# Moving the weight transfers behind the first chunk's loads, overlapping the first chunk's pieces, and multiplying by rms_g after the transpose, in a fused retention and SwiGLU kernel

## The chip, the cores and the metric

One core of a Trainium2 chip. The metric is the time of one execution on the device, in microseconds (us). The kernel before takes 300.7 us. Every run below ran on one core, beside runs of the kernel before on the same chip.

## The reference

Two operations in a row: a retention recurrence over 4 batches, 8 heads and 768 positions, then an RMS norm and a SwiGLU feed-forward network (FFN) on the 3072 rows that it gives.

```python
# attention part: B=4, H=8, S=768, D=64
for t in range(S):
    state = gamma[h] * state + outer(k[t], v[t])
    y[t] = scale * q[t] @ state
# FFN part: x is y as 3072 rows of 512; d_ff = 1536
xn  = x / sqrt(mean(x*x) + 1e-6) * rms_g
out = (silu(xn @ w_gate) * (xn @ w_val)) @ w_out
```

## The kernel before

In the views of the profile PE is TensorE, ACT is ScalarE, DVE is VectorE, POOL is GpSimd and SP is SyncE; SPq is the queue of transfers that SP issues. The sequence is cut into six chunks of 128 positions. For a chunk and a batch there are five pieces:

- **cast:** q and k to bf16, v times a decay (vp).
- **T:** transposes of q and k, and their copy out of PSUM (qkT).
- **A:** scores and the causal mask (am).
- **Y:** output and state.
- **X:** normalise (xn), transpose (xt), copy into xnT.

FFN c works on the four batches of chunk c. It has 16 slots: twelve gate and value blocks gv(n), then four down projections down(b). The pieces of chunk c+1 are emitted between these slots. The traces show each engine at its instructions in the order of emission (in experiment 12 an instruction whose input was there at 21.85 us began at 27.67, behind one that waited for its load), so the plan of slots *is* the schedule.

```python
for b in range(B):
    load(0, b)                       # q, k, v of chunk 0: 12 transfers on SP
...
g_bc = const.tile([128, DM], F32, name="g_bc")
nc.sync.dma_start(out=g_bc, in_=moe_rms_g.partition_broadcast(128))
...
for i in range(DFF // WB):           # all weights, at once, on GpSimd (fp32 in DRAM, bf16 in the tiles)
    nc.gpsimd.dma_start(out=wg_b[:, :, sl], in_=wg_v[:, :, sl])
    nc.gpsimd.dma_start(out=wv_b[:, :, sl], in_=wv_v[:, :, sl])
for i in range(3):
    nc.gpsimd.dma_start(out=wo_b[:, sl, :], in_=wo_v[:, sl, :])
...
def piece_x(c, b):
    nc.vector.scalar_tensor_tensor(out=xn, in0=x, scalar=rstd[:, b:b + 1], in1=g_bc,
                                   op0=ALU.mult, op1=ALU.mult)
    for s in range(KS):
        nc.tensor.transpose(xt_ps[:, s, :], xn[:, s * 128:(s + 1) * 128], ident)
    nc.vector.tensor_copy(xnT[:, :, b * C:(b + 1) * C], xt_ps)

def attention(c):                    # slots of FFN c-1 behind which each piece of chunk c stands
    for b in range(B):
        s[2 * b].append(lambda b=b: cast(c, b))
        s[2 * b + 1].append(lambda b=b: piece_t(c, b))
        s[2 * b + 2].append(lambda b=b: piece_a(c, b))
        s[2 * b + 3].append(lambda b=b: piece_y(c, b))
        s[12 + b].append(lambda b=b: piece_x(c, b))
    s[10].append(lambda: piece_rstd(c))    # one rstd for the four batches
...
for sl in attention(0):              # chunk 0 has no FFN beside it
    for f in sl: f()
for c in range(NCH):                 # FFN c with the pieces of chunk c+1
    ...
```

## Time and profile before

The three executions took 300.64, 300.68 and 300.84 us. The beginnings of the FFNs, taken from PE's instructions in order of time (the first g_ps matmul of each chunk), divide the profiled span of 299.4 us:

| stretch | from | length, us | what limits it |
|---|---|---|---|
| start (chunk 0's pieces) | 0 | 59.26 | transfers to 42, then a serial chain |
| FFN 0 | 59.26 | 42.99 | PE, with slow first matmuls (four fours in 6.00 us, 3.47 in FFN 1) |
| FFN 1 | 102.25 | 40.47 | PE |
| FFN 2 | 142.72 | 40.52 | PE |
| FFN 3 | 183.24 | 40.53 | PE |
| FFN 4 | 223.77 | 40.30 | PE |
| FFN 5 (no pieces beside it) | 264.07 | 35.33 | PE |

How the lines behind the table are read is told in the prediction.

### The profile page before, as it was taken

What the parts mean: (1) busy time and instruction counts of PE and PEld (TensorE: products, weight loads), DVE (VectorE), ACT (ScalarE), POOL (GpSimd) and SP (SyncE); (2) the same over time, 40 slices, a digit from 0 to 9 for tenths busy, and PEclk for the clock granted to TensorE, in tenths of its full rate; (3) what the DMA queues carried; (4) which work ended last, traced back from release to release, by engine and by line L of the source; (5) the groups of instructions that cost most, each with busy time, mean ns of one, the idle gap of its engine ahead of it and who ended that gap; (6) DMA issues with size and microseconds to landing.
All of it is one profiled execution on the core that took longest, in us unless ns stands there. A gap on an engine that the chain in (4) does not pass through costs nothing.

```text
span 299.4 us, 4437 instructions
## 1 busy us (share of the span) xinstructions
PE 242.3 (81%) x1696; PEld 122.8 (41%) x1696; DVE 141.1 (47%) x232; ACT 100.0 (33%) x186; POOL 91.2 (30%) x153
## 2 busy tenths in 40 slices
PE   0025212399999999999999999999999999999994
PEld 0014111145544454544454444545444444544441
DVE  0006405617765266873376653577544556424300
ACT  5012212034452245431445313544224453233321
POOL 8472245403337006281035350161921101000000
PEclk9999999999999999999999999999999999999999
DMA  8999999992400498002793025970110000110012
GB/s 164 191 191 192 196 197 227 219 218 44 96 3 35 129 228 171 2 0 105 182 225 53 0 73 137 219 136 1 36 71 36 2 0 2 70 70 2 1 47 93
DMA packets 84310, 30.43 MB, mean 102 GB/s; under 512 B 75457, under 2 KB 81089, under 8 KB 84289
## 3 DMA queue, kind: packets, MB, share of 16 engines
q1 hardware_dynamic: 78480, 25.43, 41.0%
q0 software_dynamic: 5808, 4.72, 9.8%
q8 instruction: 13, 0.21, 0.3%
q14 instruction: 9, 0.07, 0.1%
HBM read 28.57 MB, written 6.29 MB: 116 GB/s over the span
## 4 chain that ended last, share of the span: by engine, by line
PE 53%; DVE 17%; ACT 9%; SPq 8%; DMA 6%; issue 5%; POOL 1%; DVEq 0%; ACTq 0%; POOLq 0%
PE o_ps L259 21%; PE g_ps L248 13%; PE v_ps L251 12%; SPq L62 8%; DVE am L158 7%; DMA k_f<-in_k_dram 6%; DVE hT L254 4%; ACT xsq L188 3%; DVE x L185 3%; ACT qkT L144 3%; ACT sg L253 3%; PE xt_ps L218 2%; PE y_ps L171 2%; DVE xn L213 1%; DVE xnT L219 1%
## 5 line engine op out<-in xcount | busy, mean ns | idle before, releaser
L254 DVE TENSOR_TENSOR hT<-sg,v_ps 128x512 bf16<-128x512 bf16 x72 | 49.5, 688 | 72.5 <-PE v_ps L251 45.4
L248 PE MATMUL g_ps<-xnT,wg_b 128*128 128x512 bf16 x288 | 75.9, 387 | 3.1 <-DVE xnT L219 3.1
L251 PE MATMUL v_ps<-xnT,wv_b 128*128 128x512 bf16 x288 | 74.9, 383 | 0.0
L259 PE MATMUL o_ps<-wo_b,hT 128*128 128x512 bf16 x288 | 65.6, 379 | 0.0
L253 ACT ACTIVATE sg<-g_ps 128x512 bf16<-128x512 f32 x72 | 43.0, 597 | 63.9 <-PE g_ps L248 63.9
L198 POOL CAST st_b<-st_f 64x256 bf16<-64x256 f32 x40 | 15.9, 397 | 110.6 <-DVE st_f L197 102.5
L158 DVE TENSOR_TENSOR am<-a_ps,causal 128x512 bf16<-128x512 f32 x48 | 30.8, 682 | 33.5 <-PE a_ps L154 33.5
L251 PEld LDWEIGHTS <-wv_b 128*128 128x128 bf16 x288 | 28.5, 99 | 35.0 <-issue 1.7
L259 PEld LDWEIGHTS <-hT 128*128 128x128 bf16 x288 | 27.5, 98 | 30.4
L248 PEld LDWEIGHTS <-wg_b 128*128 128x128 bf16 x288 | 25.5, 99 | 29.1 <-DVE xnT L219 3.5
L262 ACT COPY o_sb<-o_ps 128x512 f32<-128x512 f32 x24 | 14.1, 586 | 56.5 <-PE o_ps L259 56.5
L144 ACT COPY qkT<-qk_ps 128x1024 bf16<-128x1024 bf16 x24 | 23.9, 998 | 25.0 <-PE qk_ps L142 25.0
L188 ACT ACTIVATE xsq<-x 128x512 f32<-128x512 bf16 x24 | 15.1, 630 | 49.4 <-DVE x L185 47.7
L142 PE MATMUL qk_ps<-ident,qb 128*128 128x128 bf16 x96 | 10.2, 234 | 24.4 <-POOL qb L129 24.4
L131 POOL TENSOR_TENSOR vp<-v_f,vdec 128x512 bf16<-128x512 f32 x24 | 26.8, 1117 | 8.7 <-DMA v_f<-in_v_dram 5.5
L219 DVE COPY xnT<-xt_ps 128x512 bf16<-128x512 bf16 x24 | 10.2, 425 | 31.4 <-PE xt_ps L218 31.4
L213 DVE SCALAR_TENSOR_TENSOR xn<-x,rstd,g_bc 128x512 bf16<-128x512 bf16 x24 | 23.5, 980 | 1.9 <-POOL rstd L207 1.9
L129 POOL CAST qb<-q_f 128x512 bf16<-128x512 f32 x24 | 17.0, 707 | 14.4 <-issue 8.8
L171 PE MATMUL y_ps<-vp,am 128*128 128x64 bf16 x192 | 13.6, 202 | 8.7 <-DVE am L158 5.9
L185 DVE TENSOR_TENSOR x<-y_ps,ydec 128x512 bf16<-128x512 f32 x24 | 16.6, 690 | 4.7 <-PE y_ps L171 4.1
L142 PEld LDWEIGHTS <-qb 128*128 128x128 bf16 x96 | 7.1, 105 | 25.8 <-POOL qb L129 24.6
L218 PE MATMUL xt_ps<-ident,xn 128*128 128x128 bf16 x96 | 10.2, 234 | 8.7 <-DVE xn L213 8.7
(38 smaller groups left out, 140.2 us busy)
## 6 DMA issues: line engine op xcount, KB each, us to landing
q_f<-in_q_dram SPq DMA_DIRECT2D x24, 256.0 KB, 4.8
k_f<-in_k_dram SPq DMA_DIRECT2D x24, 256.0 KB, 4.9
v_f<-in_v_dram SPq DMA_DIRECT2D x24, 256.0 KB, 4.9
out_dram<-o_sb SPq DMA_DIRECT2D x24, 256.0 KB, 2.0
wg_b<-in_moe_w_gate_dram POOLq DMA_DIRECT2D x4, 384.0 KB, 13.4
wv_b<-in_moe_w_val_dram POOLq DMA_DIRECT2D x4, 384.0 KB, 15.5
wo_b<-in_moe_w_out_dram POOLq DMA_DIRECT2D x3, 512.0 KB, 23.0
g_bc<-in_moe_rms_g_dram SPq DMA_DIRECT2D x1, 256.0 KB, 8.1
```

The source lines that it names most:

```text
L62: nc.sync.dma_start(out=x, in_=src[b].rearrange("h (c p) d -> c p h d", p=C)[c])
L131: nc.gpsimd.tensor_tensor(out=vp, in0=v_f, in1=vdec[:, c, :, None].to_broadcast([128, H, D]), op=ALU.mult)
L144: nc.scalar.copy(qkT, qk_ps)
L158: nc.vector.tensor_tensor(out=am[:, i], in0=a_ps[i], in1=causal[:, None, :].to_broadcast([128, NHP, 128]), op=ALU.mult)
L185: nc.vector.tensor_tensor(out=x, in0=y_ps, in1=ydec[:, c, :, None].to_broadcast([128, H, D]), op=ALU.mult)
L188: nc.scalar.activation(xsq, x.rearrange("p h d -> p (h d)"), AF.Square, accum_out=cur[c, "ssq"][:, b:b + 1])
L213: nc.vector.scalar_tensor_tensor(out=xn, in0=x.rearrange("p h d -> p (h d)"), scalar=cur[c, "rstd"][:, b:b + 1], in1=g_bc, op0=ALU.mult, o ...
L248: nc.tensor.matmul(g_ps, wg_b[:, s, sl], xnT[:, s, :], start=s == 0, stop=s == KS - 1)
L251: nc.tensor.matmul(v_ps, wv_b[:, s, sl], xnT[:, s, :], start=s == 0, stop=s == KS - 1)
L253: nc.scalar.activation(sg, g_ps, AF.Silu)
L254: nc.vector.tensor_tensor(out=hT[:, n, :], in0=sg, in1=v_ps, op=ALU.mult)
L259: nc.tensor.matmul(o_ps, hT[:, n, b * C:(b + 1) * C], wo_b[:, n, :], start=n == 0, stop=n == NFF - 1)
```

## The change

The intent has three parts. **Transfers:** the weights wait until chunk 0's loads are partly in (a block behind each batch's cast, the rest behind all of chunk 0), and chunk 1's loads wait for the first silus of FFN 0. **Overlap:** chunk 0's pieces are interleaved across batches, rstd is made per batch, and chunks 1 to 5 get new slots for their pieces. **rms_g:** the multiply by g moves from xn to the copy of xT out of PSUM, where g is one number per partition. Eight matmuls without a use ("hot") stand ahead of FFN 0, so that PE's slow stretch falls on them.

```diff
-    for i in range(DFF // WB):          # all weights at once
+    def load_w(i):                      # one gate and one value block
...
+        if c == 0 and b > 0:            # in cast(): a block behind the casts of batches 1, 2, 3
+            load_w(b - 1)
-        if c + 1 < NCH:
+        if 0 < c < NCH - 1:
             load(c + 1, b)
...
-        x = work.tile([128, H, D], BF16, name="x", bufs=5)
+        x = work.tile([128, H, D], F32, name="x", bufs=5)
...
-        nc.vector.scalar_tensor_tensor(
-            out=xn, in0=x..., scalar=cur[c, "rstd"][:, b:b + 1], in1=g_bc, op0=ALU.mult, op1=ALU.mult)
+        nc.vector.tensor_scalar_mul(xn, d["x"]..., d["rstd"])
...
-        nc.vector.tensor_copy(cur[c, "xnT"][:, :, b * C:(b + 1) * C], xt_ps)
+        nc.vector.tensor_tensor(out=cur[c, "xnT"][:, :, b * C:(b + 1) * C], in0=xt_ps,
+            in1=g_col[:, :, None].to_broadcast([128, KS, 128]), op=ALU.mult)
...
+    PLAN = dict(cast=(0, 2, 4, 6), t=(1, 3, 5, 7), a=(2, 4, 6, 8), y=(3, 5, 7, 9), x=(9, 11, 13, 14))
+    PLAN1 = dict(cast=(6, 7, 9, 11), t=(7, 9, 11, 13), a=(8, 10, 12, 14), y=(9, 11, 13, 15), x=(13, 14, 15, 15))
...
-    for sl in attention(0):
-        for f in sl: f()
+    for step in "C0 T0 C1 A0 T1 Y0 C2 A1 T2 X0 Y1 C3 A2 T3 X1 Y2 A3 X2 Y3".split():
+        P[step[0]](0, int(step[1]))
+    for i in range(3, DFF // WB): load_w(i)
+    for i in range(3): load_wo(i)
+    hot = fps.tile([128, GT], F32, name="hot", tag="ff")
+    for i in range(8):
+        nc.tensor.matmul(hot, ident, st_b[0]..., start=True, stop=True)
+    piece_x(0, 3)
...
+            if c == 0 and i < B:
+                load(1, i, after=mark[0, i])     # behind the silu of block i
```

Left out of this excerpt: in chunk 0 the qb casts and st_f copies move to ACT, the load buffers go from five to six, an early Silu brings the table load (1.28 us, at 48.73 before) forward, and four small transfers on ACT's queue replace the 256 KB one of g_bc.

More of the change, by code (lines that the diff above doesn't have):

```diff
@@ L45 @@
     const = ctx.enter_context(tc.tile_pool(name="const", bufs=1))
-    loads = ctx.enter_context(tc.tile_pool(name="loads", bufs=5))
+    loads = ctx.enter_context(tc.tile_pool(name="loads", bufs=6))
     work = ctx.enter_context(tc.tile_pool(name="work", bufs=3))
@@ L53, with load @@
     out_v = out.rearrange("(b c p) m -> c b p m", b=B, p=C)
+    SYNC_DEP = mybir.DependencyInfo(mybir.DependencyClass.Sync, mybir.DependencyReason.DATA)
     raw = {}
-    def load(c, b):
+    def load(c, b, after=None):
         t = []
@@ L61, in load @@
             x = loads.tile([128, H, D], F32, name=name)
-            nc.sync.dma_start(
+            i = nc.sync.dma_start(
                 out=x, in_=src[b].rearrange("h (c p) d -> c p h d", p=C)[c])
+            if after is not None:
+                tc.add_manual_dep(i.ins, after.ins.name, SYNC_DEP, reason="transfer order")
             t.append(x)
@@ L91 @@
         nc.scalar.activation(ydec[:, :, h], pos_f, AF.Exp, scale=lng[h], bias=lnscale)
-    eps4 = const.tile([128, B], F32, name="eps4")
-    nc.gpsimd.memset(eps4, 1e-6)
-    mhalf4 = const.tile([128, B], F32, name="mhalf4")
-    nc.gpsimd.memset(mhalf4, -0.5)
-    g_bc = const.tile([128, DM], F32, name="g_bc")
-    nc.sync.dma_start(out=g_bc, in_=moe_rms_g.partition_broadcast(128))
+    mhalf = const.tile([128, 1], F32, name="mhalf")
+    nc.gpsimd.memset(mhalf, -0.5)
+    warm = const.tile([128, 1], F32, name="warm")
+    nc.scalar.activation(warm, zero, AF.Silu)
+    g_col = const.tile([128, KS], F32, name="g_col")
+    for s in range(KS):
+        nc.scalar.dma_start(out=g_col[:, s:s + 1], in_=moe_rms_g[s * 128:(s + 1) * 128][:, None])
     st_f = [const.tile([128, NHP, D], F32, name=f"st_f{b}") for b in range(B)]
@@ L116, with load_wo @@
         nc.gpsimd.dma_start(out=wv_b[:, :, sl], in_=wv_v[:, :, sl])
-    for i in range(3):
+    def load_wo(i):
         sl = slice(i * 4, (i + 1) * 4)
@@ L122 @@
     cur = {}
+    mark = {}
     def cast(c, b):
@@ L128, in cast @@
         vp = work.tile([128, H, D], BF16, name="vp")
-        nc.gpsimd.tensor_copy(qb, q_f.rearrange("p h d -> p (h d)"))
+        if c == 0:
+            nc.scalar.copy(qb, q_f.rearrange("p h d -> p (h d)"))
+        else:
+            nc.gpsimd.tensor_copy(qb, q_f.rearrange("p h d -> p (h d)"))
         nc.gpsimd.tensor_copy(kb, k_f.rearrange("p h d -> p (h d)"))
@@ L187, in piece_y @@
         xsq = work.tile([128, DM], F32, name="xsq")
+        ssq = work.tile([128, 1], F32, name="ssq")
         nc.scalar.activation(xsq, x.rearrange("p h d -> p (h d)"), AF.Square,
-                             accum_out=cur[c, "ssq"][:, b:b + 1])
+                             accum_out=ssq)
+        d["ssq"] = ssq
+        piece_rstd(c, b)
         if c < NCH - 1:
@@ L194, in piece_y @@
                 if c == 0:
-                    nc.vector.tensor_copy(st_f[b][r], kv)
+                    nc.scalar.copy(st_f[b][r], kv)
                 else:
@@ L199, in piece_y, with piece_rstd @@
         d["x"] = x
-    def piece_rstd(c):
-        ssq = cur[c, "ssq"]
-        ms = work.tile([128, B], F32, name="ms")
-        nc.gpsimd.tensor_scalar(out=ms, in0=ssq, scalar1=1.0 / DM, scalar2=1e-6,
+    def piece_rstd(c, b):
+        ms = work.tile([128, 1], F32, name="ms")
+        nc.gpsimd.tensor_scalar(out=ms, in0=cur[c, b]["ssq"], scalar1=1.0 / DM, scalar2=1e-6,
                                 op0=ALU.mult, op1=ALU.add)
-        rstd = work.tile([128, B], F32, name="rstd")
-        nc.gpsimd.tensor_tensor(out=rstd, in0=ms, in1=mhalf4, op=ALU.pow)
-        cur[c, "rstd"] = rstd
+        rstd = work.tile([128, 1], F32, name="rstd")
+        nc.gpsimd.tensor_tensor(out=rstd, in0=ms, in1=mhalf, op=ALU.pow)
+        cur[c, b]["rstd"] = rstd
     def piece_x(c, b):
-        x = cur.pop((c, b))["x"]
+        d = cur.pop((c, b))
         xn = work.tile([128, DM], BF16, name="xn")
-        nc.vector.scalar_tensor_tensor(
-            out=xn, in0=x.rearrange("p h d -> p (h d)"), scalar=cur[c, "rstd"][:, b:b + 1],
-            in1=g_bc, op0=ALU.mult, op1=ALU.mult)
+        nc.vector.tensor_scalar_mul(xn, d["x"].rearrange("p h d -> p (h d)"), d["rstd"])
         xt_ps = aps.tile([128, KS, 128], BF16, name="xt_ps", tag="at")
@@ L218, in piece_x @@
             nc.tensor.transpose(xt_ps[:, s, :], xn[:, s * 128:(s + 1) * 128], ident)
-        nc.vector.tensor_copy(cur[c, "xnT"][:, :, b * C:(b + 1) * C], xt_ps)
+        nc.vector.tensor_tensor(
+            out=cur[c, "xnT"][:, :, b * C:(b + 1) * C], in0=xt_ps,
+            in1=g_col[:, :, None].to_broadcast([128, KS, 128]), op=ALU.mult)
     def begin(c):
-        cur[c, "ssq"] = work.tile([128, B], F32, name="ssq")
         cur[c, "xnT"] = work.tile([128, KS, GT], BF16, name="xnT", bufs=2)
+    PLAN = dict(cast=(0, 2, 4, 6), t=(1, 3, 5, 7), a=(2, 4, 6, 8), y=(3, 5, 7, 9), x=(9, 11, 13, 14))
+    PLAN1 = dict(cast=(6, 7, 9, 11), t=(7, 9, 11, 13), a=(8, 10, 12, 14), y=(9, 11, 13, 15), x=(13, 14, 15, 15))
     def attention(c):
@@ L228, in attention @@
         s[0].append(lambda: begin(c))
+        plan = PLAN1 if c == 1 else PLAN
+        pieces = dict(cast=cast, t=piece_t, a=piece_a, y=piece_y, x=piece_x)
         for b in range(B):
-            s[2 * b].append(lambda b=b: cast(c, b))
-            s[2 * b + 1].append(lambda b=b: piece_t(c, b))
-            s[2 * b + 2].append(lambda b=b: piece_a(c, b))
-            s[2 * b + 3].append(lambda b=b: piece_y(c, b))
-            s[12 + b].append(lambda b=b: piece_x(c, b))
-        s[10].append(lambda: piece_rstd(c))
+            for n, f in pieces.items():
+                s[plan[n][b]].append(lambda f=f, b=b: f(c, b))
         return s
@@ L252, in gv @@
             sg = ffw.tile([128, GT], BF16, name="sg")
-            nc.scalar.activation(sg, g_ps, AF.Silu)
+            mark[c, n] = nc.scalar.activation(sg, g_ps, AF.Silu)
             nc.vector.tensor_tensor(out=hT[:, n, :], in0=sg, in1=v_ps, op=ALU.mult)
@@ L269, in ffn @@
         return slots
-    for sl in attention(0):
-        for f in sl:
-            f()
+    begin(0)
+    P = dict(C=cast, T=piece_t, A=piece_a, Y=piece_y, X=piece_x)
+    for step in "C0 T0 C1 A0 T1 Y0 C2 A1 T2 X0 Y1 C3 A2 T3 X1 Y2 A3 X2 Y3".split():
+        P[step[0]](0, int(step[1]))
+    for i in range(3, DFF // WB):
+        load_w(i)
+    for i in range(3):
+        load_wo(i)
+    hot = fps.tile([128, GT], F32, name="hot", tag="ff")
+    for i in range(8):
+        nc.tensor.matmul(hot, ident, st_b[0].rearrange("p a b -> p (a b)"), start=True, stop=True)
+    piece_x(0, 3)
     for c in range(NCH):
```

## The prediction

- That the new xn takes about as long as the old xnT copy (425 ns) was the author's estimate; the trace before has no such xn.
- The xn of the trace before depends on what GpSimd does beside it. It took 0.74 us with no GpSimd instruction beside it (start 177.47) and 1.63 where a vp of 1.04 lay wholly beside it, with kb ahead and qb behind (start 172.18); where it began 0.14 ahead of vp it took 0.74 and that vp 1.50 (start 174.66). Why is not shown. Rival C's range of 0.3 to 1.2 is 0.74 and 1.63 less the 0.43 estimated for the new xn.
- "Half clock" and "cold" stand for a matmul of 512 columns in about 0.43 us instead of 0.216. At the begin of FFN 0 only these times show it: the granted clock from 59.26 to 65.26 us is 1.00 in the profile, while four fours took the 6.00 us.
- The 0.7 and 0.8 us that Part 2 charges for it are estimates, set beside the 2.7 that it names for FFN 0 before (6.00 less the 3.47 of FFN 1's first four fours gives 2.5). How they follow from it is not shown.

> **What bounds the kernel now.** I read the page's 40 slices first, because a share over the whole span would mix two quite different stages.
>
> ```profile
> PE   0025212399999999999999999999999999999994
> DMA  8999999992400498002793025970110000110012
> ```
>
> Columns are 7.5 us wide. PE is nearly idle for eight columns (60 us), then full to the end; DMA is full for the first six columns. So a start limited by transfers is followed by a stretch limited by PE. The busy time by stretch gives sizes (columns: stretch, length, PE busy (x), PEld, DVE, ACT, POOL, clock, DMA share, GB/s):
>
> ```profile
> 0.00:43.00 43.00, 8.88 (x90) 6.41 (x91) 8.19 (x15) 9.41 (x26) 21.08 (x45) 1.00 1.17 187
> 59.00:102.00 43.00, 41.70 (x288) 20.51 (x287) 23.86 (x41) 15.43 (x28) 13.89 (x22) 1.00 0.44 86
> 142.70:183.20 40.50, 39.15 (x288) 19.96 (x288) 23.84 (x40) 15.61 (x28) 13.89 (x22) 1.00 0.48 105
> 264.00:299.40 35.40, 31.25 (x144) 14.03 (x144) 8.27 (x13) 9.51 (x16) 0.00 (x0) 1.00 0.10 38
> ```
>
> The span is therefore 59.3 (attention of chunk 0 alone) + 43.0 (FFN 0) + 4 x 40.5 (FFN 1 to 4) + 35.3 (FFN 5) = 299.6. The chain that ended last shows what the 59.3 consist of:
>
> ```profile
> 16.91 7.11 SPq L62
> 24.07 17.99 DMA k_f<-in_k_dram
> 42.18 0.62 POOL kb L130
> ...
> 49.51 1.06 POOL rstd L207
> 50.59 1.10 DVE xn L213
> ...
> 58.13 0.62 PE xt_ps L218 x4
> 59.26 1.86 PE g_ps L248 x4
> 61.12 1.71 PE v_ps L251 x4
> ```
>
> Up to 42.2 it is the last batch's load; then 7.3 us of one batch's pieces, and from rstd to the FFN 9.8 us for four normalise-transpose-copy rounds in series. The first FFN matmuls take 1.86 and 1.71 us per four; later fours take 0.86.
>
> The loads' own view:
>
> ```profile
> L62 SPq DMA_DIRECT2D q_f<-in_q_dram x5: 434/908/7109, 0.8 to 40.9; - x5
> DMA to landing us min/median/max: 3.3/5.4/23.5
> ```
>
> The first load lands 3.3 us after issue, batch 3's 23.5 us after. Asking issue by issue, loads land 5.6 us apart while weights share the engines (11.2, 16.8, 22.3, 27.7, 33.6), but 1.17 us apart when alone (46 to 64 us). A weight block of 384 KB lands every 2.75 us meanwhile.
>
> [...] 5.6 against 1.17 us per load. So putting weights behind chunk 0 should help it, and weights beside chunk 1 should hurt that one. [...] about 5 us of FFN matmuls at 0.43 us each (1.71/4), then 0.216 (0.86/4). [...] Here the bf16 PSUM copy xnT takes 425 ns and every 512-column tensor_tensor about 690. I estimate the new xn as the former and the new xnT as the latter. [...] The old xn spreads from 0.74 to 1.63 us, mean 0.98[...].
>
> **Part 1: the start, 59.3 to about 35.** I walk the new instruction order with durations of this trace.
>
> Loads alone: first three at 4.1, 5.3, 6.4, then one per 1.17, so batch 1 is in by 10 and, undisturbed, batch 3 by 17. The first weight blocks leave GpSimd only after batch 1's vp, about 11. In this trace weights delayed landings 4 us after their issue (4.15 to 8.1), so from 15 the last one or two loads are slowed; v of batch 3 lands between 18 and 24, not 43.
>
> Compute is now the longer chain, because each engine works in order. ACT must do 16 Exps (to 5.3), a table load (1.28), a warm Silu and four small DMA issues, so qb of batch 0 ends near 9.2. Transposes 1.1, qkT 1.0, scores 0.7, am 1.3, Y 0.9, x 0.7, square 0.8 follow: xsq at 15.9. On GpSimd ms (0.2), rstd (0.3 to 1.0: 1.01 measured for four columns) and st_b (0.86) stand ahead of batch 2's kb and vp; that gives kb at 18 and, one round on, kb of batch 3 at 24. One round costs about 6 us, of which GpSimd works about 5 (kb 0.55, vp 1.0, two DMA issues 1.5, ms and rstd 0.5 to 1.2, st_b 0.85). From kb 3: transposes and qkT to 25.6, Y2 to 26.1, xsq2 27.6, rstd2 28.5, st_b2, X2 and Y3 to 30.5, x3 31.2, xsq3 32, rstd3 33, xn3, xt3, xnT3 35.3. The eight hot matmuls (8 x 0.43 = 3.4, 30.5 to 34) lie inside that wait. FFN 0 begins at about 35 (range 32 to 39): -24.
>
> **Part 2: FFN 0, 43.0 to about 46.** Pure PE work of a chunk is 24 x 0.865 + 48 x 0.216 + attention. One batch's attention takes 1.72 warm, by the PE's order of time in FFN 2 (T 0.45, A 0.33, Y with state and kv 0.72, X 0.22), so 6.9 for four. Sum 38.0. Before, cold matmuls added 2.7; I charge 0.7 now. Added: in the order of PE the last slot is down(3), X2, Y3, X3. Nothing lies behind Y3 to hide x 0.7, square 0.8, ms and rstd 0.5 to 1.2, xn 0.45, transposes 0.3, xnT 0.7 and handoffs: about 5 us in which PE is idle before FFN 1, and 0.8 of half clock after it. Chunk 1's loads (from the first silu, 36.5) meet w3 and wo, which GpSimd issues at 34 to 38: at 5.6 us each k of batch 0 lands near 47.4 and v at 53, then 1.17 each. T of batch 1 is wanted at 54.8 and gets kb at 56: 1.5. w3 is wanted at 51 and wo near 60, both in time. 38.0+0.7+5+0.8+1.5 = 46.0: +3.0.
>
> **Part 3: FFN 1 to 4, 40.5 to about 42.2 each.** X moves from behind down(0..3) to slots 9, 11, 13 and 14. What goes: 0.68 of PE idle at each chunk's end, where the last xnT was waited for. What comes: X0 now stands behind gv(9) and X1 behind gv(11). DVE works in order, so xn stands behind that slot's hT, which needs the v_ps that has just ended.
>
> ```profile
> 167.11 0.69 DVE L254 TENSOR_TENSOR hT<-sg,v_ps 128x512 bf16<-128x512 bf16 x1
> 167.19 0.38 PE L171 MATMUL y_ps<-vp,am 128*128 128x64 bf16 x7 [0.16 <-DVE am L158]
> ```
>
> gv(9) ends at 166.84; hT occupies DVE from 167.11, next start 0.6 later, xn to 168.15, transposes at 168.2. Against Y3 running from 167.19 that loses 1.0 beyond the transposes' own 0.22 (moved, not added). X1: 0.27 + 0.6 + 0.43 + 0.05 = 1.3. Net 2.35 - 0.68 = +1.7 per chunk, four chunks +6.7.
>
> **Part 4: what is off the path.** The Silu table load (1.28) lay beside rstd. Dropping g_bc frees 256 KB of transfer behind the loads. qb and st_f of chunk 0 move to ACT. Per chunk DVE saves 4 x 0.55 on xn and pays 4 x 0.27 on xnT, but is busy only 24 of 40.5. FFN 5 is unchanged: 35.3.
>
> **Sum.** 35 + 46.0 + 4 x 42.2 + 35.3 = 285.1 span; the profiled execution had 299.4 span for about 300.7, so +1.3: 286.4 us, rounded to **286.5**, 4.7% less.
>
> **Rivals.** (A) *The start becomes purely a matter of loads* and the pieces overlap better than I walk: FFN 0 at about 29, FFN 0 without a data stall, period kept at 40.5. Then 29 + 44 + 162 + 35.3 + 1.3 = 272. For it: batch 3 can be in at 18. Against it: the in-order queue on GpSimd, which puts rstd and st_b ahead of the next batch's kb. (B) *The transfers are only moved*: three weight blocks still catch batch 3's loads, and chunk 1's loads, beside w3 and wo at 5.6 us each, stall FFN 0 by 10 instead of 1.5: 286.5 + 8.5 = 295. For it: the 5.6 us spacing is measured. Against it: wo should be done by 53, after which 1.17 holds. (C) *The order costs more*: xn [...] (0.74 to 1.6) in X0 and X1 adds 0.3 to 1.2 twice per chunk, 2.4 to 9 in four chunks: 289 to 295.5. Against it: GpSimd is idle from 163.4 to 168.9 in this trace.
>
> **Range and chances.** The start may err by 4 either way, FFN 0 by 3, the four periods by 3 together; B and C push up, A down. 80%: 278 to 293. Faster by 2% means under 294.7: only B or C in full, or both in part, spoil that: 0.92. Same 0.07, slower 0.01.
>
> **What would show it.** Start: first g_ps at 32 to 39, the chain before it running through POOL and ACT pieces rather than one 18 us DMA; v_f landings with a maximum under 12 us before 25. If GpSimd waits for DMA instead, my step on its order is wrong. Hot: the first g_ps four under 1.3 us. FFN 0: a PE wait of about 5 us on xnT just before FFN 1, and a wait of kb or vp for DMA in FFN 0 of 1 to 3 us. Period: 42.2, PE waiting for xn twice per chunk about 1.3 each, no wait for xnT at the end; 40.5 or less would refute Part 3. New xn near 430 ns and xnT near 690. What would make the total wrong: a data stall in FFN 0 of over 5 us, or a start under 31.

## The result, and the profile after

The changed kernel takes **295.93 us** (median of four executions, 294.84 to 296.61), against 300.66 of the kernel before in the same rounds. The ratio of the fast runs is 0.9845 (95% interval 0.9806 to 0.9885). A ratio here is the mean time of one kernel's fast runs over the mean of the other's in the same rounds, so it is not quite the ratio of the medians that are quoted. By the 2% rule this is "same". The predicted 286.5, and its range of 278 to 293, were too low: three times as large a gain had been forecast.

First the slices of the page after the change (40 columns of 7.3 us; PEclk is the clock that was granted to PE, in tenths):

```profile
PE   0364798699939998899996899996999978999994
PEclk9999999799969999999999999999999999999999
DMA  9999699999999400028920129900120000110012
```

PE now starts in the second column and works from the fifth. But it has a hole in the twelfth, a dent in the seventh and eighth and shallower ones later, and the clock falls in the eighth and the twelfth. DMA, which was full without a break for nine columns before (the prediction reads six from its own line), has a gap at the fifth. The busy time by stretch (columns as in the prediction) answers to the lines of before:

```profile
36.08:85.50 49.42, 40.12 (x284) 20.60 (x289) 23.68 (x40) 15.82 (x28) 18.94 (x34) 0.94 1.11 207
85.50:129.90 44.40, 40.49 (x282) 20.31 (x288) 23.16 (x40) 15.02 (x27) 18.11 (x33) 0.96 0.42 79
173.70:216.10 42.40, 38.66 (x283) 19.78 (x287) 23.15 (x40) 15.61 (x28) 14.96 (x28) 1.00 0.50 100
```

PE's busy time per FFN is about the same as before, but each stretch is longer, and in the first two the clock was 0.94 and 0.96. As a table, with the stretches measured as before, the forecast beside them:

| stretch | before | forecast | after | after less before | after less forecast |
|---|---|---|---|---|---|
| start | 59.26 | 35.0 | 36.08 | -23.18 | +1.1 |
| FFN 0 | 42.99 | 46.0 | 49.42 | +6.43 | +3.4 |
| FFN 1 | 40.47 | 42.2 | 44.49 | +4.02 | +2.3 |
| FFN 2 | 40.52 | 42.2 | 43.58 | +3.06 | +1.4 |
| FFN 3 | 40.53 | 42.2 | 42.58 | +2.05 | +0.4 |
| FFN 4 | 40.30 | 42.2 | 42.24 | +1.94 | 0 |
| FFN 5 | 35.33 | 35.3 | 35.01 | -0.32 | -0.3 |
| span | 299.4 | 285.1 | 293.4 | -6.0 | +8.3 |

So the start gained nearly all that was hoped for, 23 us of 24, and the six FFNs gave 17 of it back. The chain that ended last shows the new start, and then where FFN 0 waits (columns: start, length, what; a "four" below is the four matmuls that make one g_ps or v_ps):

```profile
4.82 5.19 DMA v_f<-in_v_dram
10.41 0.63 ACT qb L139
...
24.95 0.62 POOL kb L142
...
32.04 3.03 PE hot L298 x7
35.34 0.70 DVE xnT L233
36.08 1.04 PE g_ps L264 x4
...
38.17 14.95 DMA k_f<-in_k_dram
53.24 0.63 POOL kb L142
...
55.18 1.50 PE v_ps L267 x4
...
77.14 3.99 DMA out_dram<-o_sb
...
81.71 0.73 ACT xsq L203 x2
```

The 18 us transfer at the start is gone, and the pieces on ACT, GpSimd, VectorE and PE take its place. A 15 us transfer of chunk 1 has appeared inside FFN 0, and behind it v_ps takes 1.50 us where 0.86 is normal. At the end of FFN 0 the chain runs through an output transfer, for which ACT waits (more on this in experiments 2 and 3). The longest waits of PE, from its own instructions in order of time (in brackets how long PE had been idle, and for what):

```profile
53.92 0.40 PE L156 MATMUL qk_ps<-ident,kb 128*128 128x128 bf16 x4 [3.64 <-POOL kb L142]
84.11 0.61 PE L232 MATMUL xt_ps<-ident,xn 128*128 128x128 bf16 x4 [3.75 <-DVE xn L229]
113.04 0.40 PE L232 MATMUL xt_ps<-ident,xn 128*128 128x128 bf16 x4 [1.25 <-DVE xn L229]
118.94 0.40 PE L232 MATMUL xt_ps<-ident,xn 128*128 128x128 bf16 x4 [1.37 <-DVE xn L229]
162.53 0.40 PE L232 MATMUL xt_ps<-ident,xn 128*128 128x128 bf16 x4 [2.38 <-DVE xn L229]
```

The first is chunk 1's data, the second the end of FFN 0, the third and fourth the pair that recurs in every later chunk (X0 behind gv(9), X1 behind gv(11)), and the fifth is one of that pair that came out longer.

### The profile page after: what moved, and what is told of

It is laid out like the page before. It is cut to its first block, busy times and chain, and to the rows that moved or that the text cites. A ratio compares the mean times of both kernels' runs of the same rounds, so it can differ in the third digit from the quotient of the medians.

```text
span 293.4 us, 4497 instructions
## 1 busy us (share of the span) xinstructions
PE 242.3 (83%) x1673; PEld 123.9 (42%) x1704; DVE 135.3 (46%) x224; ACT 105.6 (36%) x199; POOL 96.1 (33%) x184
## 4 chain that ended last, share of the span: by engine, by line
PE 51%; DVE 17%; ACT 10%; DMA 8%; issue 7%; POOL 4%; SPq 2%; ACTq 0%; DVEq 0%; POOLq 0%
PE o_ps L275 19%; PE v_ps L267 11%; PE g_ps L264 11%; DVE am L172 6%; DMA k_f<-in_k_dram 5%; ACT xsq L203 4%; DVE hT L270 4%; DVE x L199 4%; ACT qkT L158 3%; ACT sg L269 3%; PE xt_ps L232 3%; DVE xn L229 2%; DMA v_f<-in_v_dram 2%; PE qk_ps L156 2%; SPq L64 2%
## 5 line engine op out<-in xcount | busy, mean ns | idle before, releaser
L270 DVE TENSOR_TENSOR hT<-sg,v_ps 128x512 bf16<-128x512 bf16 x72 | 49.5, 688 | 86.0 <-PE v_ps L267 61.5
L264 PE MATMUL g_ps<-xnT,wg_b 128*128 128x512 bf16 x272 | 73.4, 386 | 2.8 <-DVE xnT L233 1.6
L275 PE MATMUL o_ps<-wo_b,hT 128*128 128x512 bf16 x281 | 63.9, 379 | 0.5 <-issue 0.2
L220 POOL TENSOR_SCALAR ms<-ssq 128x1 f32<-128x1 f32 x24 | 4.8, 202 | 123.8 <-ACT xsq L203 123.8
L233 DVE TENSOR_TENSOR xnT<-xt_ps,g_col 128x512 bf16<-128x512 bf16 x24 | 16.6, 692 | 36.3 <-PE xt_ps L232 36.3
L203 ACT ACTIVATE xsq<-x 128x512 f32<-128x512 f32 x24 | 15.1, 630 | 43.9 <-DVE x L199 43.9
L143 POOL TENSOR_TENSOR vp<-v_f,vdec 128x512 bf16<-128x512 f32 x24 | 25.3, 1053 | 3.5 <-DMA v_f<-in_v_dram 3.5
L232 PEld LDWEIGHTS <-xn 128*128 128x128 bf16 x96 | 7.1, 105 | 24.9 <-DVE xn L229 22.2
L142 POOL CAST kb<-k_f 128x512 bf16<-128x512 f32 x24 | 15.1, 627 | 6.5 <-DMA k_f<-in_k_dram 6.4
L199 DVE TENSOR_TENSOR x<-y_ps,ydec 128x512 f32<-128x512 f32 x24 | 16.5, 686 | 1.0 <-PE y_ps L185 0.7
L229 DVE TENSOR_SCALAR xn<-x,rstd 128x512 bf16<-128x512 f32 x24 | 14.6, 609 | 4.4 <-POOL rstd L223 4.4
```

Source lines behind the costliest of these rows:

```text
L143: nc.gpsimd.tensor_tensor(out=vp, in0=v_f, in1=vdec[:, c, :, None].to_broadcast([128, H, D]), op=ALU.mult)
L199: nc.vector.tensor_tensor(out=x, in0=y_ps, in1=ydec[:, c, :, None].to_broadcast([128, H, D]), op=ALU.mult)
L203: nc.scalar.activation(xsq, x.rearrange("p h d -> p (h d)"), AF.Square, accum_out=ssq)
L229: nc.vector.tensor_scalar_mul(xn, d["x"].rearrange("p h d -> p (h d)"), d["rstd"])
L264: nc.tensor.matmul(g_ps, wg_b[:, s, sl], xnT[:, s, :], start=s == 0, stop=s == KS - 1)
L270: nc.vector.tensor_tensor(out=hT[:, n, :], in0=sg, in1=v_ps, op=ALU.mult)
```

## The experiments

Twelve kernels ran; all gave the right result. "Start" below is the begin of FFN 0. Lengths of stretches come from each run's own trace, and times are medians of four executions unless said otherwise. The kernel before took 300.07, 300.38 and 300.25 us.

### 1. The x pieces back in their old slots

```diff
-    PLAN = dict(..., x=(9, 11, 13, 14))
+    PLAN = dict(..., x=(12, 13, 14, 15))
```

> One edit: in the plan for chunks 2 to 5 the x pieces go back to slots 12 to 15, behind the down projections. My theory (X0 and X1 behind gv(9) and gv(11) stop PE 1.25 and 1.37 us per chunk, and 2.38 us once where xn met GpSimd's casts): the periods of FFN 2 to 4 fall from 43.7, 42.5, 42.3 to about 40.8 each, FFN 1 from 44.4 to 43, waits of xt_ps for xn in those chunks vanish, and a wait for xnT of about 0.95 us comes at each chunk's end; time 295.9 to about 289. Rival (PE's stop there is absorbed by waits it would have had anyway, and the rest of the loss is the clock): periods change by under 0.5, time stays within 294 to 297.

Measured: 288.37 us (ratio to before 0.9598). FFN 1 to 4 took 43.45, 40.90, 40.90 and 40.68 (changed kernel: 44.49, 43.58, 42.58, 42.24). The waits for xn in them are gone, and at each chunk's end stands this instead (PE's instructions in order of time):

```profile
170.19 1.04 PE L264 MATMUL g_ps<-xnT,wg_b 128*128 128x512 bf16 x3 [0.79 <-DVE xnT L233]
```

The new slots for X are therefore a loss of about 7.5 us. The rival, that PE's stop there would be absorbed, has fallen. The edit moves four entries of a table of slots; the waits name the first two. This give-back is at least as large as that of the transfers, for which experiment 5 gets 6.3 us.

### 2. w_out held back until chunk 1's second batch is in

```diff
-    for i in range(3): load_wo(i)            # behind all of chunk 0
+        if c == 1 and b == 1:                # in cast()
+            for i in range(3): load_wo(i)
```

> One edit: the three w_out transfers are issued on GpSimd behind chunk 1's second batch cast, no longer right behind the last gate and value block. My theory (chunk 1's first loads are slowed by w_out beside them, k lands 14.9 us after issue): k of batch 0 of chunk 1 lands before 47, the 3.64 us wait of its transposes for kb at 50 us goes, and with it the half clock after it (about 1.6); FFN 0 falls from 49.4 to about 44.5, time from 295.9 to about 291. Rival (the loads are late because they are issued only behind the first silu, contention is minor): k lands less than 3 us earlier and the wait stays above 1.5; time 294 to 296. A second rival: w_out now arrives too late and down(0) waits; time up.

Measured: 295.69 us (0.9854), so no gain in time, yet the landing moved just as expected. The load of k for chunk 1's batch 0, in the changed kernel and then in this one (issue, and time from issue to landing):

```profile
L64 SPq DMA_DIRECT2D k_f<-in_k_dram x1: 703/703/703, 38.2 to 38.2; - x1
DMA to landing us min/median/max: 14.9/14.9/14.9
```

```profile
L64 SPq DMA_DIRECT2D k_f<-in_k_dram x1: 582/582/582, 38.7 to 38.7; - x1
DMA to landing us min/median/max: 5.8/5.8/5.8
```

So the contention is real: 9 us of that landing was w_out (14.9 less 5.8). The wait for kb and the slow matmuls behind it are gone. But the FFN still took 47.9 us, because two other waits took their place, one on PE and one on ACT:

```profile
64.79 1.02 PE L278 MATMUL o_ps<-wo_b,hT 128*128 128x512 bf16 x4 [1.31 <-DMA wo_b<-in_moe_w_out_dram]
...
80.24 0.58 ACT L281 COPY o_sb<-o_ps 128x512 f32<-128x512 f32 x1 [6.84 <-DMA out_dram<-o_sb]
```

w_out came too late for down(0). And the fourth output copy waited for one of three buffers: the output transfers stand in SP's queue behind chunk 2's loads, so none of them was issued before 76.1. The square of batch 3 stands behind that copy on ACT, so the chain at the end of FFN 0 grew, and PE's wait for xn there rose from 3.75 to 6.18 us. The changed kernel has the same wait of the fourth copy, 4.41 us long (ACT in order of time):

```profile
81.23 0.59 ACT L278 COPY o_sb<-o_ps 128x512 f32<-128x512 f32 x1 [4.41 <-DMA out_dram<-o_sb]
```

A further 1.7 us was lost in FFN 2, and it belongs to the clock. The stretches of 3 us after its long wait for xn show a granted clock (third number from the end) of 0.70 and 0.73:

```profile
161.00:164.00 3.00, 2.78 (x13) 1.30 (x13) 1.82 (x2) 0.00 (x0) 1.84 (x3) 0.70 0.00 0
164.00:167.00 3.00, 3.00 (x11) 1.19 (x11) 0.00 (x0) 0.58 (x1) 0.00 (x0) 0.73 0.04 18
```

The changed kernel has the same wait (2.38 us, against 2.37 here) in the same FFN and kept a clock of 1.00 behind it. So a wait of that length sometimes costs the clock and sometimes not.

### 3. No matmuls ahead of FFN 0

```diff
-    hot = fps.tile([128, GT], F32, name="hot", tag="ff")
-    for i in range(8):
-        nc.tensor.matmul(hot, ident, ..., start=True, stop=True)
```

> One edit: the eight matmuls without a use, ahead of FFN 0, are left out. My theory: they keep the clock of PE at full for FFN 0; without them the first g_ps and v_ps fours take 1.7 each [...] and FFN 0 loses 2 to 3 us; start unchanged within 0.3; time 295.9 to about 298. Rival: the clock depends on the pieces of chunk 0 as well (PE now over half busy from 11 us on), and FFN 0 starts warm without them: time unchanged within 0.5.

Measured: 296.15 us (0.9861), no slower than noise. My theory missed, but so did the rival, which held that the FFN would start warm. The first g_ps and v_ps fours ran at half clock again (four of them took 5.17 us, 36.32 to 41.49, instead of 3.46), so FFN 0 was indeed slower at first. What swallowed it is the wait at 50 us, which is set by the landing of chunk 1's k and not by PE:

```profile
54.06 0.40 PE L156 MATMUL qk_ps<-ident,kb 128*128 128x128 bf16 x4 [1.82 <-POOL kb L142]
```

It was 3.64 with the hot matmuls, and PE resumed at 53.92 there and at 54.06 here. Whatever is saved ahead of a wait for a transfer is waited for.

The same happens a second time. Behind the shorter wait PE kept its full clock (the g_ps and v_ps fours behind it took 0.86 us each), so it was through down(3) at 77.84 instead of 79.29. Yet FFN 1 began at 85.77 instead of 85.50, because the fourth output copy, ahead of batch 3's square on ACT, now waited longer for an output transfer (ACT in order of time):

```profile
81.51 0.59 ACT L278 COPY o_sb<-o_ps 128x512 f32<-128x512 f32 x1 [6.13 <-DMA out_dram<-o_sb]
```

### 4. Chunk 1's batch 3 one slot earlier

```diff
-    PLAN1 = dict(cast=(6, 7, 9, 11), t=(7, 9, 11, 13), a=(8, 10, 12, 14), y=(9, 11, 13, 15), ...
+    PLAN1 = dict(cast=(6, 7, 9, 10), t=(7, 9, 11, 12), a=(8, 10, 12, 13), y=(9, 11, 13, 14), ...
```

> One edit: in chunk 1's plan batch 3's cast, T, A and Y are one slot earlier (T3 behind down(0), A3 behind T3 and down(1), Y3 behind down(2)), x unchanged. My theory (nothing hides batch 3's chain from Y to xnT behind down(3): PE is idle 5 us at the end of FFN 0, and runs at half clock [...]): the wait of xt_ps for xn at about 84 us goes, at most 1 us of wait for xnT is left, FFN 1 starts warm; FFN 0 falls from 49.4 by 4 to 5, FFN 1 from 44.4 to about 42.3; time 295.9 to about 290. Rival: A3 then waits for qkT, or T3 for batch 3's load, and gives half of it back: time 292.5 to 294.

Measured: 292.28 us (0.9732), 3.65 less than the changed kernel. FFN 0 took 47.35 (49.42 before this edit) and FFN 1 42.56 (44.49), whose first matmuls ran at full clock (four fours in 3.45 us, 83.56 to 87.01). So the chain behind Y3 did cost both its idle time and the clock behind it. The gain in FFN 0 is smaller than expected: 1.61 us of wait for xn and 0.78 for xnT are left, because xn and the transposes of X2 and X3 still alternate behind down(3). The time is nearer to the rival's range (292.5 to 294), which it misses by 0.2, than to my 290, though not for the rival's reason: no wait of 0.4 us or more for qkT or for batch 3's load appears among PE's waits of FFN 0.

### 5. Weights issued earlier

```diff
-        if c == 0 and b > 0: load_w(b - 1)
+        if c == 0 and b == 1:
+            for i in range(3): load_w(i)
+        if c == 0 and b == 2: load_w(3)
+        if c == 0 and b == 3:
+            for i in range(3): load_wo(i)
```

> One edit: GpSimd issues three gate and value blocks behind batch 1's cast of chunk 0 (it stood idle there from 12.8 to 17.5 us), the fourth behind batch 2's and w_out behind batch 3's, instead of a block per batch and the rest behind all of chunk 0. My theory (the engines stood partly empty between 20 and 35 us, because the issues waited in GpSimd's order, and these bytes then met chunk 1's loads): w_out has landed by about 46 instead of 52.5, k of chunk 1's batch 0 lands by 47 instead of 53.1, the wait of 3.64 for kb shrinks under 1, w_out is in time (unlike with w_out held back); start 36 to 37; FFN 0 falls by 3 to 5 unless output copies take it back at its end; time 295.9 to about 292. Rival: the earlier blocks now slow batch 3 of chunk 0 (its v would land near 26 instead of 21) and the start is 2 or more later: no gain.

Measured: 289.67 us (0.9659), 6.3 less than the changed kernel, more than expected. w_out landed by 41.6 (at 28.3, the last issue, plus 13.3), k of chunk 1's batch 0 at 43.9:

```profile
L64 SPq DMA_DIRECT2D k_f<-in_k_dram x1: 582/582/582, 38.4 to 38.4; - x1
DMA to landing us min/median/max: 5.5/5.5/5.5
```

No wait for kb of 0.4 us or more is left, the fourth output copy waits for PE and no longer for an output transfer, and FFN 0 took 43.18 instead of 49.42. The start stayed at 36.34, although batch 3's v now landed 12.0 us after its issue instead of 8.5. The DMA engines had had room between 20 and 35 us (in the changed kernel they moved 114 GB/s there, 187 in the first 15 us), and the rival falls. Here the weights were best late enough to spare the loads ahead of them and early enough to spare those behind them.

### 6. The x piece cut in two

```diff
-    PLAN = dict(..., x=(9, 11, 13, 14))
+    PLAN = dict(..., xn=(11, 12, 13, 13), xt=(12, 13, 14, 14))
```

The multiply xn and the transposes with their copy become two pieces; the first is issued on VectorE a slot ahead of the second. Chunks 2 to 5 are changed, which stand beside FFN 1 to 4.

> The x piece of chunks 2 to 5 is cut in two: the VectorE multiply is issued a slot ahead (slots 11, 12, 13, 13), the transposes and their copies behind down(0), (1), (2), (2). My theory (both the stop for xn and the stop for the last xnT are matters of order): neither wait is left in FFN 1 to 4; periods about 40.1 (the 40.9 of the run with the old slots less 0.8 of wait for xnT), FFN 1 about 42.5; time 295.9 to about 285.5, 3 us under the run with the old slots. Rival: with transposes of two batches behind down(2) PE waits for PSUM buffers or VectorE is late for hT of the next chunk: no better than the old slots, about 288.4.

Measured: 283.61 us (0.9456). FFN 2, 3 and 4 took 39.95, 39.95 and 39.73, and FFN 1 took 41.52, still with slow first matmuls (four fours in 5.02 us, 85.37 to 90.39, behind a wait of 3.64 for xn). No wait for xn or xnT of 0.4 us or more is left in FFN 1 to 4. The time is 1.9 us under the 285.5 expected, and the rival falls. Both the stop for xn and the stop for the last xnT were matters of order alone. This one edit is worth 12 us, more than the whole change gave.

### 7 and 8. Chunk 0's pieces in the old order, with and without the hot matmuls

```diff
-    "C0 T0 C1 A0 T1 Y0 C2 A1 T2 X0 Y1 C3 A2 T3 X1 Y2 A3 X2 Y3"
+    "C0 T0 A0 C1 Y0 T1 A1 C2 Y1 T2 A2 C3 Y2 T3 A3 Y3 X0 X1 X2"
```

> One edit: chunk 0's pieces in the order of the kernel before (cast, T, A, Y batch by batch with the next T behind Y, X of three batches behind Y3), transfers and all else as in the changed kernel. It tells what the overlap is worth apart from the order of transfers. My theory (loads are in by 21 us, so the start is a chain of pieces through in-order engines, and the overlap shortens that chain): FFN 0 begins 2 to 3 us later, at 38 to 39, but half of that is taken back by the shorter wait for kb at 50 us, which is set by the loads; time 296 to 298. Rival (the start is set by loads and GpSimd's round, the order of pieces is nothing): start within 0.7, time unchanged.

Measured: 297.39 us (0.9900). The start is 43.15, 7.1 later than with the overlap, so my 2 to 3 was too small; yet the time is only 1.5 longer, since no wait for kb of 0.4 us or more is left (FFN 0 took 43.88 instead of 49.42). Part of the 7.1 are the hot matmuls, which stand ahead of the last transposes and here are waited for; hence the second run.

> The changed kernel with chunk 0's pieces in the order of before and without the eight matmuls, which stood in front of the last transposes there and were waited for. It leaves of the start the order of transfers and the rms_g part alone. My theory: FFN 0 begins at about 40.5 instead of 43.2, with its first matmuls at half clock; so of the 23.2 us that the start lost, some 18.7 come from the transfers and 4.5 from the overlap; time 296 to 299. Rival: the matmuls cost nothing there, 43.

Measured (one execution, state unknown): 296.55 us, start 41.30. Of the 23.2 us that the start lost, 5.2 therefore come from interleaving the pieces, and 18.0 (59.26 less 41.30) from all the rest: not only the order of transfers and the rms_g part, as the expectation has it, but also rstd per batch, the work moved to ACT and the early table load, which this run keeps. These were not separated. The stretch is read from one execution.

### 9. Only rms_g, on the kernel before

The edit is the parts of the diff that concern xn and xnT, with g_col in place of g_bc and the fp32 x; rstd, plan, start and the other transfers as before.

> The kernel before with only the rms_g part of the change: per-partition columns of g multiplied as xT leaves PSUM, x in fp32, xn a tensor_scalar; transfers, order and plan as before. My theory: nearly nothing. xn falls from 0.98 to about 0.54, xnT rises from 0.42 to 0.69, the wait for xnT at each chunk's end rises by 0.27 (five times 1.35 in all), the four serial rounds of the start lose about 4 x 0.2: time 300.1 to between 299.5 and 301.5. Rival (the fp32 x or the broadcast costs more on VectorE in the interleaved part): over 302.

Measured: 302.05 us (1.0060, interval 1.0034 to 1.0086), a little above the stated range and at the edge of the rival's "over 302". FFN 1 took 40.73 (40.47 before), from a wait for xnT of 0.79 instead of 0.52 at its end, which recurs at each chunk's end; the start came out at 59.68 instead of 59.26, where a gain of about 0.8 had been expected. The growth of each period is the longer wait for xnT that my theory named, not the rival's load on VectorE. The multiply on the way out of PSUM is therefore a small loss of its own, as long as xnT is waited for.

### 10. All edits together

```diff
+        # weights as in experiment 5
+    PLAN  = dict(cast=(0, 2, 4, 6), t=(1, 3, 5, 7), a=(2, 4, 6, 8),  y=(3, 5, 7, 9),  xn=(11, 12, 13, 13), xt=(12, 13, 14, 14))
+    PLAN1 = dict(cast=(3, 5, 7, 9), t=(4, 6, 8, 10), a=(5, 7, 9, 11), y=(6, 8, 10, 12), xn=(11, 12, 13, 13), xt=(12, 13, 14, 14))
-            o_sb = ffw.tile([128, DM], F32, name="o_sb")
+            o_sb = ffw.tile([128, DM], F32, name="o_sb", bufs=6)
```

> The changed kernel with the edits that the runs point to: weights issued early, x cut in two for chunks 1 to 5 with the transposes behind the down projections, chunk 1's plan three slots behind the later chunks' one (batch 3's Y behind down(0), not behind down(3)), and six output buffers. My theory: start 36 as before; FFN 0 without a wait for loads and without the chain at its end, 39.5 to 41; FFN 1 warm, 40; FFN 2 to 4 40 each; FFN 5 35; span 36.3 + 40.5 + 160 + 35 = 272, time about 274. Rival (chunk 1's loads are not there at slot 4, 45 us): a wait of 1 to 3 us for kb in FFN 0 and half clock behind it, 276 to 279.

Measured: **272.68 us** (272.51 to 272.90), ratio 0.9076 to the kernel before (interval 0.905 to 0.9102). The stretches are 36.25, 39.91, 39.94, 39.94, 39.95, 39.72 and 34.99. In the slices of its page PE is full from FFN 0 on and the clock never falls:

```profile
PE   0156689999999999999999999999998999999994
PEclk9999999999999999999999999999999999999999
```

This version beats both kernels. It also closes the account: with the start of the changed kernel kept, taking away the waits named above brings every FFN to 40.0 us or less. What the six output buffers add was not run alone; in experiment 5 no copy at the end of FFN 0 waited for a buffer with three.

### 11. All edits, without the hot matmuls

The edit is that of experiment 3, on the combined kernel.

> The combined kernel without the eight matmuls ahead of FFN 0. In the changed kernel leaving them out cost nothing because the time that they save was waited for loads at 50 us. My theory: where no such wait is left they are worth what the slow first matmuls cost, so this is 1.5 to 3 us slower than the combined kernel. Rival (FFN 0 is bound by its loads here too): the same within 0.7, with the wait for kb in FFN 0 shorter by as much as the start of FFN 0 is slower.

Measured: 275.30 us (0.9159), 2.6 more than the combined kernel. The start is 36.57, and FFN 0 took 42.04 instead of 39.91, so 2.1 of it is the half clock at the begin of FFN 0 (the first four fours took 5.59 us, 36.57 to 42.16, instead of 3.46). The same eight matmuls were worth nothing in experiment 3, where transfers are waited for afterwards.

### 12. All edits, with batch 2's and 3's casts ahead

```diff
-    "C0 T0 C1 A0 T1 Y0 C2 A1 T2 X0 Y1 C3 A2 T3 X1 Y2 A3 X2 Y3"
+    "C0 T0 C1 A0 C2 T1 Y0 A1 C3 T2 X0 Y1 W3 A2 T3 X1 Y2 O0 A3 X2 Y3"     # W3, O0: issue of the rest of the weights
```

> The combined kernel with batch 2's and 3's casts in chunk 0 issued ahead of the previous batches' rstd and st_b on GpSimd, and a block of weights behind each cast again. It tests the claim of the prediction that the start is set by GpSimd's order (kb of the next batch but one behind rstd and st_b). My theory: kb of batch 2 comes at about 13.5 instead of 19.9 and of batch 3 near 20 instead of 25.6, FFN 0 begins at 31 to 33 instead of 36; with weights later, chunk 1's first loads meet w_out again and part is waited for: time 2 to 4 us under the combined kernel. Rival (the start is a chain through ACT and VectorE as well, which the earlier casts don't shorten): FFN 0 begins at 35 or later.

Measured: 276.96 us (0.9212), 4.3 *more* than the combined kernel, the start at 39.55. kb of batches 2 and 3 came at 12.9 and 19.7, as wanted (19.5 and 25.2 in the combined kernel). But vp of batch 3, from now on ahead of batch 1's rstd in GpSimd's order, stood there waiting for its load (GpSimd in order of time):

```profile
25.01 1.04 POOL L143 TENSOR_TENSOR vp<-v_f,vdec 128x512 bf16<-128x512 f32 x1 [4.72 <-DMA v_f<-in_v_dram]
```

Two blocks of weights, issued at 11.2 and 15.0, met that load. FFN 0 did begin later than 35, as the rival said, but not because of the chain that it named. Moving an instruction ahead also moved its wait ahead of everything behind it on that engine: batch 1's ms, the step ahead of rstd, had its input at 21.85 us and began at 27.67, behind that vp and two issues of weights. Whether the start can be shortened by casts ahead of rstd with the weights later still was not tried.

## Why the prediction was right or wrong

**Part 1, the start, was right.** FFN 0 began at 36.08, forecast 35 with a range of 32 to 39. The steps are there too: batch 2's kb is at 19.29 (forecast 18) and batch 3's at 24.95 (forecast 24), and xnT of batch 3 starts at 35.34. The loads of v in the first 30 us landed at most 8.5 us after issue (23.5 was the longest of the loads before). Experiments 7 and 8 split the gain into 5.2 for interleaving the pieces and 18.0 for all the rest; rms_g alone gave nothing of it (experiment 9). The step on GpSimd's order is right as a reading of the chain, but undoing that order, as experiment 12 did it, made the start later.

**Part 2, FFN 0, failed at the wait for chunk 1's loads.** Forecast 46.0, measured 49.42. The failed step reads "k of batch 0 lands near 47.4", with a wait of 1.5 us at batch 1's T only (its own figures, 54.8 to 56, give 1.2). k landed at 53.1 (38.2 plus 14.9), and PE waited 3.64 already at batch 0's T. I had let q land about 5 us after its issue and spaced the others by 5.6; but q already took 11.3 us. Experiment 2 puts 9 us of k's landing down to w_out beside it. Behind that wait PE ran at half clock (granted clock 0.54 from 55 to 58 us), which was not in the sum at all. The stretch from 54.15 to 59.62 (two blocks at 1.73 and an A piece at 0.33 by the rates of the prediction, 3.8 in all) took 5.47, so 1.7 more.

The chain at the end was forecast at 5; from the end of down(3), 79.29, to 85.50 it is 6.21, of which 1.1 is PE's own work, so 5.1. That the two agree is partly luck. The forecast chain has no output transfer in it, and the measured one waits for one: batch 3's square began at 81.71, behind the fourth output copy. In experiment 5, where that copy does not wait for a transfer, the chain takes 4.1 (74.31 to 79.52, less 1.1). So about 1 us belongs to outputs that stand in SP's queue behind loads, for which the prediction had no term. Experiment 3 shows that this wait also hides what is lost ahead of it: there the half clock behind the wait for kb was absent, and FFN 0 was no shorter (49.45).

PE's work with its small waits was put too low, at 38.0: experiment 5's 43.18 less that chain leaves 39.1. With this, 39.1 + 3.64 + 1.7 + 5.1 is 49.5, close to the 49.42 measured. The charge of 0.7 for a cold begin of FFN 0 was not needed, and the 0.8 falls into FFN 1.

**The clock after the end of FFN 0** was charged with 0.8. The first four fours of FFN 1 took 5.36 us (85.50 to 90.86) instead of 3.46, so it was 1.9, and this is most of FFN 1's excess of 2.3. Experiment 4, where that wait is shorter, has FFN 1 at 42.56. The prediction charged slow matmuls at the begin of FFN 0 and behind this one wait, and should have asked the same for each new wait in its list. Behind the waits for kb and xn, 3.64 and 3.75 us, the granted clock of this trace fell to 0.54 (55 to 58 us) and 0.50 (84 to 88 us). Behind the 1.61 us that are left in experiment 4 the first four fours took 3.45, so nothing was lost there.

**Part 3, the later FFNs, was right in FFN 3 and 4 and short in FFN 2.** Forecast 42.2; measured 42.58 and 42.24, with waits of 1.25 and 1.37 for xn (forecast 1.0 and 1.3; for the wait for xnT that goes it counted 0.68 where the profile has 0.52). Experiments 1 and 6 show that these waits are the cause. In FFN 2, X1 waited 2.38. There xn took 1.25 us beside a vp on GpSimd (GpSimd's and VectorE's instructions in order of time):

```profile
161.16 1.04 POOL L143 TENSOR_TENSOR vp<-v_f,vdec 128x512 bf16<-128x512 f32 x1
```

```profile
161.23 1.25 DVE L229 TENSOR_SCALAR xn<-x,rstd 128x512 bf16<-128x512 f32 x1
```

The shortest xn of the trace is 0.477 us, its median 0.538. GpSimd's vp began 0.07 ahead and xn ended 0.28 after it. That is rival C in one chunk of four. In FFN 1 the same two met the other way round. xn began ahead of vp and took 0.60, and it was vp that grew, from 1.04 to 1.21 us:

```profile
118.28 0.60 DVE L229 TENSOR_SCALAR xn<-x,rstd 128x512 bf16<-128x512 f32 x1
```

```profile
118.57 1.21 POOL L143 TENSOR_TENSOR vp<-v_f,vdec 128x512 bf16<-128x512 f32 x1
```

By what the two slow each other is not shown, and no run isolated it. Of the 1.0 us by which the wait exceeds that of FFN 1, the longer xn is 0.65; the rest is an hT that began later ahead of it, and why it did is not shown. The prediction argued against C from GpSimd's idle time up to 168.9 in the trace before. That covers X0's place only: at X1's, behind gv(11), where hT begins at 171.57, GpSimd had started the next chunk's casts at 171.09 in that same trace.

**Part 4** held for FFN 5, which changed by 0.3 us. That rms_g is off the path held only roughly: experiment 9 has it at +0.6%, from the wait for xnT. The new xnT takes 692 ns, as estimated, and the new xn 538 ns (median; 0.48 with no GpSimd instruction beside it, as at 78.27) instead of 430.

**The rivals.** A (the pieces overlap better than walked) did not come. B was the right worry and happened by about a third: the stall was 3.64, with 1.7 of half clock behind it, where B had 10. C happened in one chunk. They did not exclude one another, and I priced them as if each came alone; and what I had charged for the clock behind waits was 0.8 for the whole kernel, where it slowed PE by 1.7 and 1.9.

**The sum.** Against the forecast span of 285.1 the start is 1.1 over, FFN 0 3.4, FFN 1 2.3, FFN 2 1.4 and the rest 0.1 together: 8.3. The remaining 1.2 up to 295.93 is outside the profiled span: the profiled execution took 2.03 us more than its span instead of the 1.3 assumed (which set the span of one execution against the time of others; the profiled one of the kernel before took 301.07, 1.7 more than its span), and the median of the four is 0.5 above it. Executions of the changed kernel also scatter by 0.6%, and their mean clock goes with it (0.988 in the fastest, 0.977 in the slowest), which fits waits that cost the clock only sometimes; that this is the reason was not tested.

## What to carry to other kernels

Draw up the stretches of a kernel and compare each one. A change that rightly empties the start can be eaten by slots and transfers that it moved elsewhere: here 23 us were gained and 17 given back. Issue a small VectorE result that PE needs one slot ahead of the PE instruction, behind work that hides it: in experiment 6 this took away waits of 1.25 to 2.38 us and was worth 12 us in all. Put a transfer late enough to spare what is needed before it, early enough not to meet what is needed after it (6.3 us in experiment 5). Look at what stands in a queue ahead of the outputs: with three buffers an output copy on ACT waited 4.41 us for outputs behind loads in the changed kernel, and 6.84 with w_out held back. And count a PE wait with the clock that can follow it: waits of 3.64 and 3.75 us cost 1.7 and 1.9 more in the changed kernel. A wait of 2.37 (w_out held back) was followed by a granted clock of 0.70 and 0.73 in the next two stretches of 3 us, one of 2.38 in the changed kernel by 1.00, so at that length it can cost and need not.
